# Attention and a gated feed-forward layer on one core: sums of squares in place of maxima, and another planned order

## The chip, the cores and the metric

The kernel runs on one core of one Trainium2 chip. The metric is the device time of one execution in microseconds (us). The engines are TensorE (PE in the rows, its weight loads PEld), VectorE (DVE), ScalarE (ACT), GpSimd (POOL) and SyncE (SP), which issues all transfers of this kernel. Engines run side by side, each takes its own instructions strictly in order, and they wait for one another by semaphores.

## The reference

```python
# q, k, v: (8, 8, 576, 64); f: (8, 8, 576); w_in: (512, 2048); w_out: (2048, 512)
scores = scale * np.matmul(q, k.transpose(0, 1, 3, 2))
cum = np.cumsum(np.log(np.clip(f, 0.0001, 1.0)), axis=-1)
decay = cum[:, :, :, None] - cum[:, :, None, :]
scores = np.where(causal, -1000000000.0, scores + decay)
attn = softmax(scores)                    # row maximum subtracted
out = np.matmul(attn, v)                  # (8, 8, 576, 64)
x = out.transpose(0, 2, 1, 3).reshape(4608, 512)
h = x @ w_in
y = (h * np.cos(h)) @ w_out               # (4608, 512)
```

The weights come as 64-bit floats, the rest as 32-bit floats.

## The kernel before

Work is cut into 32 attention steps, one for each batch and pair of heads (numbers n = 0 to 31), and 16 feed-forward units, two for each batch (320 and 256 tokens). For a pair the kernel computes scores in blocks (L668, L823, L825, L826), adds the mask and takes row minima of the negative (VectorE, L676 or L837), takes exponentials with row sums (ScalarE, L686 or L842), transposes the result (TensorE, L639, for n below 4, by a DMA later), multiplies by v (L713 or L892) and writes x as a high and a low half-precision word (`xh`, `xl`). A unit multiplies x by the first weights in four chunks of four groups (L922, evacuated by ScalarE, L928), applies h cos h (`L937` is the gate's first VectorE operation, a sine on ScalarE follows at L941), and multiplies by the second weights (L968).

Before any of it the weights are prepared. `stage` loads a tile of 128 x 512 64-bit words into a raw buffer (rings `h`, three buffers, for the first weights, and `g`, five buffers, for the second) and makes 32-bit floats of it with three VectorE operations (L472, L476, L480). `bound` sums the absolute values of a tile (ScalarE, L491) and writes the element-wise result, which nobody reads, into a buffer of the ring `ot`. That ring has one buffer, which the outputs and one reduction use too. From the sums `allmax` makes a bound over all partitions (a matmul with ones, L427) and `emit_scale` a power of two by which the tile is scaled and split into two half-precision words (ScalarE L501, VectorE L508). `prep_vscale` does the same for v of each batch: it loads v again in four tiles (ring `stage`, two buffers) and takes the largest absolute value of each with VectorE (L565).

The scores of the first pairs read a buffer of `q32`, loaded from q and k (L609) and from the rows of the decay (L610). For n below 4 this buffer comes out of the ring `g`, so it takes turns with the second weights' tiles. The decay's rows go through DRAM (`cum_d`).

No order is written by hand. Every step is recorded as an operation with an engine, a cost, a priority and the buffers that it reads and writes; a planner (`Plan.order`) simulates the engines and sets one order for each. Its knobs are at the top of the file: `PW1`, `PW2` and `VS0` are priorities of the preparation of the first and second weights and of v of the first batch, `HOLDV`, `HOLDW`, `HOLDX` and `HOLDR` keep loads back until a planned time, and `LEAD` puts the units after their attention. While TensorE is planned to wait, in the first 200 us of the plan, the planner puts in filler matmuls (448 columns, into a bank that is about to be overwritten, L1034), so that it stays busy:

```python
if o.fill and t < FILL:
    a = max([free[e]] + [x.end + 0.25 for x in o.bank])
    if t - a > 0.5:
        o.pads = pe.pad(a, t - 0.2 + PADX)
```

The number of fillers is fixed in the program; how long the wait is on the chip is not.

Of the kernel before, what the change touches and what calls it, by code (L numbers as in the profile page):

```python
# [24 lines left out]
P = 128  # L25
# [11 lines left out]
PW1, PW2 = (-0.95, 1.5, 3.05, 4.0), (2.6, 2.3)  # L37
VS0 = -1.0
# [4 lines left out]
LEAD = 1.0  # L43
HOLDV, HOLDW, HOLDR, HOLDX = 12.0, 20.0, 25.0, 12.0
# [46 lines left out]
PADX = 0.0  # L91
# [42 lines left out]
class Plan:  # L134
# [108 lines left out]
    def forward(self):  # L243
# [8 lines left out]
        t, dma_free, table, span = 0.0, 0.0, None, 0.0  # L252
        pe, port = Clock(), dict.fromkeys(SHARED, 0.0)
        while len(out) < len(self.ops):
# [10 lines left out]
            for e, q in avail.items():  # L265
                if q and free[e] <= t + 1e-9:
# [5 lines left out]
                    if e == "PE":  # L272
                        o.pads = 0
                        if o.fill and t < FILL:
                            a = max([free[e]] + [x.end + 0.25 for x in o.bank])
                            if t - a > 0.5:
                                o.pads = pe.pad(a, t - 0.2 + PADX)
                        end = pe.run(t, o.cost, o.moving)
# [38 lines left out]
def c_act(n, psum=False, aps=0):  # L317
    return (0.052 if psum else 0.093) + n / 1200.0 + 0.093 * aps
# [19 lines left out]
def fox_moe_kernel(ctx: ExitStack, tc: tile.TileContext, qkT, vp, fT, w1, w2, out):  # L338
# [72 lines left out]
    def emit_scale(m2, s, r, u):  # L411
        V.tensor_scalar(m2, m2, float(2.0 ** -40), None, op0=ALU.max)
        V.tensor_scalar(u, m2.bitcast(I32), 0x7F800000, None, op0=ALU.bitwise_and)
        V.tensor_scalar(s.bitcast(I32), u, -1, 268 << 23, op0=ALU.mult, op1=ALU.add)
        V.tensor_scalar(r.bitcast(I32), u, -(14 << 23), None, op0=ALU.add)
# [41 lines left out]

    def stage(w, k, src, pr):

        n = 1024 if wide else 512  # L460
        rb = ring("raw", [P, n], I32, tag=RAWS[w])
        raw = rb.get
        wb = [WB[w, at(w, k) + 1].part(j) for j in range(2)]
# [25 lines left out]
    def bound(w, k, am, ab, pr):  # L489
        junk = ring("junk", [P, 512], BF16, tag="ot")  # L490
        op("ACT", c_act(512, aps=1), lambda: A.activation(junk.get(), wide_of(w, k), AF.Abs, accum_out=am),  # L491
           reads=[WB[w, at(w, k) + 1].part(j) for j in range(2)], writes=[ab, junk], prio=pr)

    def wide_of(w, k):
        return WS_[w][:, at(w, k) + 1].rearrange("p a c -> p (a c)").bitcast(F32)
# [64 lines left out]
    def prep_vscale(b, pr):  # L560
        mx = sm([P, NP], F32, "vmx")
        for p in range(NP):
            st = ring("vst", [P, 640], F32, tag="stage")
            op("SP", T_DGE, lambda st=st, p=p: dma(st.get(), vp[b, p]), writes=[st], prio=pr, size=4 * P * 640, hold=HOLDV * (1 + 2 * b))
            op("DVE", c_dve(640), lambda st=st, p=p: V.tensor_reduce(mx.get()[:, p:p + 1], st.get(), axis=AX.X, op=ALU.max,  # L565
               apply_absolute_value=True), reads=[st], writes=[mx], prio=pr, port=False)
        m1, m2, u = sm([P, 1], F32, "vm1"), sm([P, 1], F32, "vm2"), sm([P, 1], I32, "vu")
        s, r = sm([P, 1], F32, "vs"), sm([P, 1], F32, "vr")
        op("DVE", c_dve(4), lambda: V.tensor_reduce(m1.get(), mx.get(), axis=AX.X, op=ALU.max), reads=[mx], writes=[m1], prio=pr)
        allmax(m1.get, 1, [m1], m2.get, [m2], pr)  # L570
        op("DVE", 0.53, lambda: emit_scale(m2.get(), s.get(), r.get(), u.get()), writes=[m2, s, r], prio=pr)
        vs[b] = (s, r)
# [492 lines left out]
```

## Time and profile before

| | |
|---|---|
| three runs, us | 1089.32, 1091.78, 1100.14 |
| median, us | 1091.78 |
| profiled execution, us | 1095.38 |
| its span, first to last instruction, us | 1093.5 |
[...]
| TensorE, VectorE, ScalarE, GpSimd busy, us | 1057.3, 812.3, 832.3, 180.0 |

The profiled execution is 3.6 us above the median. Busy time counts an instruction of TensorE up to its modelled end, and filler matmuls as work.

### The profile page before, as it was taken

How to read it: one execution, taken by the hardware profiler on the slowest of the kernel's cores; microseconds unless marked ns; L12 is line 12 of the kernel's file. 1: busy time of each engine (PE TensorE's matmuls, PEld its weight loads, DVE VectorE, ACT ScalarE, POOL GpSimd, SP SyncE). 2: the span in 40 equal slices, each digit the busy share in tenths (PEclk: the TensorE clock that was granted, in tenths of full speed). 3: DMA queues.
4: the chain of work that ended last, by engine and by line, in shares of the span. 5: the costliest groups of instructions: out<-in, count | busy, mean ns of one | idle time of the engine just before them, and what ended most of it. 6: DMA issues, size and time to landing. Idle time of an engine off the chain costs nothing. (4 is left out here: it accounts for less than half of the span.)

```text
span 1093.5 us, 23483 instructions
## 1 busy us (share of the span) xinstructions
PE 1057.3 (97%) x8978; PEld 848.6 (78%) x8978; DVE 812.3 (74%) x1790; ACT 832.3 (76%) x1731; POOL 180.0 (16%) x284
## 2 busy tenths in 40 slices
PE   8799997989999999999999999999999999999998
PEld 4587875778777887788778887778778887788787
DVE  5889999778695869778786869677786868762613
ACT  2457899698887979788897979788897979762522
POOL 1000001032213221312212221311222221100000
PEclk9779998999999999999999999999999999999999
DMA  8856334776658465877666565867667564430000
GB/s 289 269 148 220 85 79 102 161 177 124 151 146 197 97 143 116 201 135 147 146 162 167 109 139 120 192 128 164 141 167 163 101 152 96 95 60 20 7 19 20
DMA packets 256279, 146.37 MB, mean 134 GB/s; under 512 B 223336, under 2 KB 231528, under 8 KB 256168
## 3 DMA queue, kind: packets, MB, share of 16 engines
q1 hardware_dynamic: 256168, 144.88, 56.5%
q8 instruction: 70, 1.15, 0.4%
q14 instruction: 41, 0.34, 0.1%
HBM read 72.11 MB, written 10.62 MB: 76 GB/s over the span
## 5 line engine op out<-in xcount | busy, mean ns | idle before, releaser
L968 PE MATMUL hp<-g,W2s 128*128 128x256 f16 (+1 forms) x3072 | 389.4, 287 | 0.0
L922 PE MATMUL hp<-xh,W1s 128*128 128x256 f16 (+1 forms) x2048 | 381.1, 286 | 5.3 <-ACT h L928 5.1
L922 PEld LDWEIGHTS <-W1s 128*128 128x128 f16 x3072 | 294.7, 98 | 83.5 <-issue 7.2
L968 PEld LDWEIGHTS <-W2s 128*128 128x128 f16 x3072 | 297.2, 98 | 75.8 <-issue 0.3
L922 PE MATMUL hp<-xl,W1s 128*128 128x256 f16 (+1 forms) x1024 | 292.6, 286 | 0.0
L863 DVE SCALAR_TENSOR_TENSOR PS<-pa,ri,PS 128x576 f16<-128x576 f32 (+2 forms) x280 | 142.2, 544 | 32.9 <-ACT PS L859 32.3
L842 ACT ACTIVATE pa<-pa,nb 128x448 f32<-128x448 f32 (+2 forms) x280 | 141.5, 506 | 28.1 <-DVE nb L837 22.7
L837 DVE CUSTOM_DVE_ANT_0 pa<-pa,mask 128x448 f32<-128x448 f32 (+1 forms) x280 | 133.4, 505 | 19.7 <-PE pa L826 15.8
L859 ACT ACTIVATE PS<-pa,ri 128x576 f16<-128x576 f32 (+2 forms) x280 | 137.7, 542 | 11.6 <-DVE ri L850 6.0
L847 POOL TENSOR_SCALAR ri<-L 128x1 f32<-128x1 f32 (+1 forms) x168 | 55.7, 331 | 481.8 <-ACT pa L842 460.1
L928 ACT ACTIVATE h<-hp 128x320 f32<-128x320 f32 (+1 forms) x256 | 101.9, 419 | 43.3 <-PE hp L922 42.8
L943 DVE TENSOR_TENSOR h<-h,r 128x1280 f32<-128x1280 f32 (+1 forms) x64 | 87.8, 1371 | 41.9 <-ACT r L941 41.6
L951 DVE TENSOR_TENSOR g<-h,g 128x1280 f16<-128x1280 f32 (+1 forms) x64 | 90.8, 1419 | 22.0 <-ACT g L950 22.0
L939 DVE SCALAR_TENSOR_TENSOR r<-r,m_b,h 128x1280 f32<-128x1280 int32 (+1 forms) x64 | 99.0, 1546 | 1.2
L941 ACT ACTIVATE r<-r,halfpi,m_inv 128x1280 f32<-128x1280 f32 (+1 forms) x64 | 86.2, 1347 | 16.0 <-DVE r L939 15.4
L825 PE MATMUL pa<-QK 128*128 128x288 f32 (+4 forms) x288 | 92.1, 332 | 1.5 <-DVE ri L850 1.3
L771 POOL TENSOR_TENSOR QK<-stage,QK 64x576 fp32r<-64x576 f32 x48 | 76.3, 1590 | 83.1 <-ACT QK L766 47.8
L892 PE MATMUL pa<-pt,vv 128*64 128x256 f16 (+2 forms) x1512 | 78.5, 254 | 9.2 <-DMA pt<-PS 3.9
L950 ACT CAST g<-h 128x1280 f16<-128x1280 f32 (+1 forms) x64 | 74.0, 1157 | 17.1 <-DVE h L943 16.6
L892 PEld LDWEIGHTS <-vv 128*64 128x64 f16 x1512 | 69.4, 110 | 22.0 <-issue 16.5
L937 DVE TENSOR_SCALAR r<-h,m_a 128x1280 int32<-128x1280 f32 (+1 forms) x64 | 54.3, 848 | 43.2 <-ACT h L928 42.3
L826 PE MATMUL pa<-QC 68*128 68x288 f32 (+4 forms) x288 | 76.4, 304 | 0.0
(112 smaller groups left out, 1133.6 us busy)
## 6 DMA issues: line engine op xcount, KB each, us to landing
stage<-in_dram SPq DMA_DIRECT2D x48, 576.0 KB
stage<-in_dram SPq DMA_DIRECT2D x32, 320.0 KB
v<-in_dram SPq DMA_DIRECT2D x32, 320.0 KB
h<-in_dram SPq DMA_DIRECT2D x16, 512.0 KB
g<-in_dram SPq DMA_DIRECT2D x16, 512.0 KB
QC<-QK SPq DMA_DIRECT2D x48, 144.0 KB
out_dram<-ot SPq DMA_DIRECT2D x32, 160.0 KB
out_dram<-ot SPq DMA_DIRECT2D x32, 128.0 KB
```

The source lines that it names most:

```text
L825: T.matmul(c, hi[:, 0, isl], hi[:, 1, d], start=True, stop=False)
L837: op("DVE", c_dve(w) + 0.008, lambda view=view, ib=ib, o=o, w=w, mk=mk, c=c: V.tensor_tensor_reduce(out=view(ib, o, w), in0=view(ib, o, w) ...
L842: op("ACT", c_act(w, True, 2), lambda view=view, ib=ib, o=o, w=w, c=c: A.activation(view(ib, o, w), view(ib, o, w), AF.Exp, bias=nb.get()[ ...
L859: op("ACT", c_act(w, True, 1), lambda view=view, ib=ib, o=o, w=w, c=c, out_=out_: A.activation(out_(0), view(ib, o, w), AF.Copy, scale=ri. ...
L863: op("DVE", c_dve(w) + 0.06, lambda view=view, ib=ib, o=o, w=w, c=c, out_=out_: V.scalar_tensor_tensor(out_(1), view(ib, o, w), ri.get()[: ...
L892: T.matmul(d, vv.get()[:, jb, hd, kv], m, start=first and x == 0, stop=last and x == 2)
L922: T.matmul(hp.get()[:, 0:w_], WS_[1][:, at(1, 4 * c + cb), w, fs], x.get(), start=(n == 0), stop=(n == 11))
L928: op("ACT", c_act(w_, True), lambda hp=hp, k=k: A.activation(h.get()[:, k, 0:w_], hp.get()[:, 0:w_], AF.Copy, scale=float(2.0 ** -24)), re ...
L939: op("DVE", c_dve(N) + 0.045, lambda: V.scalar_tensor_tensor(fl(r), fl(r).bitcast(I32), b1.get()[:, c:c + 1], fl(h), op0=ALU.mult, op1=ALU ...
L943: op("DVE", c_dve(N), lambda: V.tensor_tensor(fl(h), fl(h), fl(r), op=ALU.mult), reads=[r], writes=hk, prio=pr)
L951: op("DVE", c_dve(N), lambda: V.tensor_tensor(gx(1), fl(h), gx(0), op=ALU.subtract), reads=[*hk, gh], writes=[gl], prio=pr, alt=("POOL", 0 ...
L968: T.matmul(po.get()[:, 0:w_], WS_[2][:, at(2, 4 * c + k), w, msl], gh.get()[:, i, k, 0:w_], start=(n == 0), stop=(n == 47))
```

## The change

The element-wise result of a weight tile's sum goes into 256 more words at the end of the tile's own raw buffer, in place of the shared buffer of `ot`. The sum is now one of squares. For the first two batches (`VACT = 2`) the maxima of v on VectorE become sums of squares on ScalarE, with the tile overwritten by its squares, and each tile's result is a part of its own. `emit_scale` halves the exponent where it is given a sum of squares. The planner starts TensorE at 2.5, puts in fillers from a planned wait of 0.3 on and up to its end, and has other priorities and holds. Its order is another from the first instructions on.

```diff
-PW1, PW2 = (-0.95, 1.5, 3.05, 4.0), (2.6, 2.3)
-VS0 = -1.0
+PW1, PW2 = (-0.95, 1.5, 4.05, 3.0), (3.6, 3.3)
+VS0 = 1.5
...
-LEAD = 1.0
-HOLDV, HOLDW, HOLDR, HOLDX = 12.0, 20.0, 25.0, 12.0
+LEAD = 2.5
+HOLDV, HOLDW, HOLDR, HOLDX = 0.0, 0.0, 25.0, 18.0
...
-PADX = 0.0
+PADG, PADE, PE0 = 0.3, 0.0, 2.5
+VACT = 2
...
+        free["PE"] = PE0
...
-                            if t - a > 0.5:
-                                o.pads = pe.pad(a, t - 0.2 + PADX)
+                            if t - a > PADG:
+                                o.pads = pe.pad(a, t - PADE)
...
+        if sq:
+            V.tensor_scalar(m2, m2, float(2.0 ** -80), float(2.0 ** 126), op0=ALU.max, op1=ALU.min)
+            V.tensor_scalar(u, m2.bitcast(I32), 1, 0x7F800000, op0=ALU.logical_shift_right, op1=ALU.bitwise_and)
+        else:
+            V.tensor_scalar(m2, m2, float(2.0 ** -40), None, op0=ALU.max)
+            V.tensor_scalar(u, m2.bitcast(I32), 0x7F800000, None, op0=ALU.bitwise_and)
...
-        rb = ring("raw", [P, n], I32, tag=RAWS[w])
+        rb = ring("raw", [P, n + 256], I32, tag=RAWS[w])
         raw = rb.get
+        raws[w, k] = rb
...
-        junk = ring("junk", [P, 512], BF16, tag="ot")
-        op("ACT", c_act(512, aps=1), lambda: A.activation(junk.get(), wide_of(w, k), AF.Abs, accum_out=am),
-           reads=[WB[w, at(w, k) + 1].part(j) for j in range(2)], writes=[ab, junk], prio=pr)
+        rb = raws[w, k]
+        op("ACT", c_act(512, aps=1), lambda: A.activation(rb.get()[:, -256:].bitcast(BF16), wide_of(w, k), AF.Square, accum_out=am),
+           reads=[WB[w, at(w, k) + 1].part(j) for j in range(2)], writes=[ab, rb], prio=pr)
...
-            op("DVE", c_dve(640), lambda st=st, p=p: V.tensor_reduce(mx.get()[:, p:p + 1], st.get(), axis=AX.X, op=ALU.max,
-               apply_absolute_value=True), reads=[st], writes=[mx], prio=pr, port=False)
+            if b < VACT:
+                op("ACT", c_act(640, aps=1), lambda st=st, p=p: A.activation(st.get(), st.get(), AF.Square, accum_out=mx.get()[:, p:p + 1]),
+                   reads=[st], writes=[mx.part(p), st], prio=pr)
+            else:
+                op("DVE", c_dve(640), lambda st=st, p=p: V.tensor_reduce(mx.get()[:, p:p + 1], st.get(), axis=AX.X, op=ALU.max,
+                   apply_absolute_value=True), reads=[st], writes=[mx.part(p)], prio=pr, port=False)
```

Three places of the order. The changed file's line numbers are higher by 8 to 16 than those before for the same statement.

On SP, ahead of the load of the second head of the first pair, before (`g_395` with L609 and L610 is that load, `h_` and `g_` from `in_3` and `in_4` are weight tiles, `stage_` a tile for v's bound, `cum_d` the decay):

```order
L482 DMA h_311<-in_3_dram 128x1024
L455 DMA cum_d_105<-pt3_136 56x2x576 x2
L482 DMA g_321<-in_4_dram 128x1024
L482 DMA h_361<-in_3_dram 128x1024
L769 DMA QC0_82<-cum_d_105 4x2x576
L769 DMA QC1_83<-cum_d_105 4x2x576
L482 DMA g_381<-in_4_dram 128x1024
L482 DMA h_386<-in_3_dram 128x1024
L564 DMA stage_388<-in_1_dram 128x640
L609 DMA g_395<-in_0_dram 64x2x576
L610 DMA g_395<-cum_d_105 4x2x576
```

The same stretch of SP now (`g_294` is the second head's buffer, `v2_` is v itself):

```order
L493 DMA h_163<-in_3_dram 128x1024
L626 DMA g_112<-cum_d_105 4x2x576
L635 DMA v2_168<-in_1_dram 128x640
L493 DMA g_171<-in_4_dram 128x1024
L575 DMA stage_176<-in_1_dram 128x640
L493 DMA h_181<-in_3_dram 128x1024
L635 DMA v2_281<-in_1_dram 128x640
L625 DMA g_294<-in_0_dram 64x2x576
L626 DMA g_294<-cum_d_105 4x2x576
L625 DMA g_298<-in_0_dram 64x2x576
L626 DMA g_298<-cum_d_105 4x2x576
L448 DMA cum_d_105<-pt3_115 56x2x576
```

The load has moved ahead of the large decay writes and of five weight tiles.

On TensorE, after the first head's scores, before (L668 scores, L427 the reduction of v's bound, L639 transposes):

```order
L668 MATMUL pa1_289<-g_112 128x320
L668 MATMUL pa1_289<-g_112 128x192
L427 LDWEIGHTS ones_78
L427 MATMUL hp_329<-dg_326,ones_78 128x128
L639 MATMUL hp_331<-eyef_76,PS3_84 128x128 x4
L639 MATMUL hp_340<-eyef_76,PS3_84 128x128 x4
```

And now, from the last of 24 fillers (L1050) that follow the first head's scores (L684 scores, L435 the reduction, L655 transposes):

```order
L1050 MATMUL pa1_328<-mask_66,ones_78 128x448
L684 MATMUL pa1_328<-g_294 128x448
L684 MATMUL pa1_328<-g_294 128x64
L684 MATMUL pa2_359<-g_294 128x288 x2
L684 MATMUL pa1_364<-g_294 128x320
L684 MATMUL pa1_364<-g_294 128x192
L684 MATMUL pa1_368<-g_298 128x448
L684 MATMUL pa1_368<-g_298 128x64
L435 LDWEIGHTS ones_78
L435 MATMUL hp_373<-dg_324,ones_78 128x128
L655 MATMUL hp_375<-eyef_76,PS3_84 128x128 x4
```

The second head's scores, which came after the first head's transposes and 33 fillers, now come before the reduction.

On ScalarE, from the start, before (L446 the decay's logarithm, L491 sums of weight tiles, L686 the first exponentials):

```order
L446 ACTIVATE vv_119<-vv_119 64x576
L491 ACTIVATE ot_132,ma_106<-W1s_98 128x512
L491 ACTIVATE ot_150,ma_106<-W1s_98 128x512
L491 ACTIVATE ot_164,ma_106<-W1s_98 128x512
L491 ACTIVATE ot_277,ma_106<-W1s_98 128x512
L686 ACT_TABLE_LOAD
L686 ACTIVATE PS3_84,L_294<-pa1_176,nb_284 128x448
```

And now (L577 the squares of v's tiles, L502 those of weight tiles, L702 the exponentials):

```order
L454 ACTIVATE vv_119<-vv_119 64x576
L577 ACTIVATE stage_121,vmx_138<-stage_121 128x640
L502 ACTIVATE g_117,am2_107<-W2s_99 128x512
L502 ACTIVATE h_125,ma_106<-W1s_98 128x512
L577 ACTIVATE stage_136,vmx_138<-stage_136 128x640
L502 ACTIVATE g_129,am2_107<-W2s_99 128x512
L502 ACTIVATE h_145,ma_106<-W1s_98 128x512
L577 ACTIVATE stage_159,vmx_138<-stage_159 128x640
L502 ACTIVATE g_154,am2_107<-W2s_99 128x512
L502 ACTIVATE h_163,ma_106<-W1s_98 128x512
L702 ACT_TABLE_LOAD
L702 ACTIVATE PS3_84,L_291<-pa1_185,nb_283 128x448
```

Three squares of v and two sums more stand ahead of the first exponential, and tiles of both weights alternate.

## Rows read from the trace of the kernel before

**Rows 1.** The page, busy us, share of the span and instructions of each engine.
```profile
PE 1057.3 (97%) x8978; PEld 848.6 (78%) x8978; DVE 812.3 (74%) x1790; ACT 832.3 (76%) x1731; POOL 180.0 (16%) x284
```

**Rows 2.** Stretches: length, busy us by engine, granted clock, DMA share, GB/s.
```profile
core 0: us, PE busy (x) PEld busy (x) DVE busy (x) ACT busy (x) POOL busy (x), PEclk, DMA share, GB/s
0.00:24.00 24.00, 21.70 (x100) 10.70 (x101) 11.20 (x20) 6.05 (x11) 4.70 (x22) 1.00 0.84 272
44.00:66.00 22.00, 21.66 (x75) 17.08 (x76) 13.10 (x39) 11.41 (x37) 0.51 (x3) 0.53 0.57 207
66.00:131.00 65.00, 62.27 (x438) 52.20 (x436) 63.46 (x190) 50.65 (x145) 3.21 (x15) 1.00 0.55 161
250.00:950.00 700.00, 689.52 (x6209) 562.61 (x6208) 542.07 (x1187) 595.46 (x1203) 152.58 (x205) 1.00 0.64 143
```

**Rows 3.** Order of time, VectorE and ScalarE: start, length, instruction, [idle before].
```profile
203.27 0.74 DVE L937 TENSOR_SCALAR r<-h,m_a 128x1024 int32<-128x1024 f32 x1
...
215.05 0.38 ACT L928 ACTIVATE h<-hp 128x256 f32<-128x256 f32 x1 [3.30 <-PE hp L922]
```

**Rows 4.** Stretches again, each from the span's start.
```profile
0.00:66.00 66.00, 55.50 (x234) 35.86 (x235) 43.26 (x105) 25.54 (x71) 5.51 (x27) 0.79 0.74 245
0.00:131.00 131.00, 117.77 (x669) 88.06 (x670) 106.72 (x295) 76.19 (x215) 8.72 (x42) 0.90 0.65 203
0.00:203.30 203.30, 184.54 (x1178) 136.30 (x1179) 176.95 (x464) 141.80 (x350) 14.98 (x58) 0.92 0.60 170
0.00:215.00 215.00, 196.24 (x1281) 145.05 (x1282) 183.70 (x473) 146.86 (x356) 15.28 (x60) 0.92 0.61 171
```

**Rows 5.** Order of time on TensorE, the first 52 us.
```profile
2.30 21.43 PE L1034 MATMUL pa<-mask,ones 128*128 128x448 bf16 x98 [2.30 <-POOL ones L361]
23.57 2.97 PE L668 MATMUL pa<-g 68*128 68x448 f32 x12
32.02 0.27 PE L427 MATMUL hp<-dg,ones 128*128 128x128 bf16 x1 [5.48 <-DVE dg L424]
...
44.34 6.74 PE L668 MATMUL pa<-g 68*128 68x288 f32 x16 [2.71 <-DMA g<-in_dram]
```

**Rows 6.** Order of time in SP's DMA queue: when loads were issued.
```profile
14.06 0.74 SPq L610 DMA_DIRECT2D g<-cum_d  x1
...
24.36 0.42 SPq L482 DMA_DIRECT2D g<-in_dram  x1
31.43 0.36 SPq L482 DMA_DIRECT2D h<-in_dram  x1
...
36.62 0.59 SPq L609 DMA_DIRECT2D g<-in_dram  x1
```

**Rows 7.** VectorE's groups up to 131 us: count, busy us, mean ns, idle before.
```profile
L476 DVE SCALAR_TENSOR_TENSOR W1s<-h,W1s 128x512 int32<-128x512 int32 x16 | 11.0, 685 | 0.1
...
L472 DVE TENSOR_SCALAR W1s<-h 128x512 int32<-128x512 int32 x16 | 6.9, 432 | 7.0 <-DMA h<-in_dram 7.0
...
L565 DVE TENSOR_REDUCE vmx<-stage 128x1 f32<-128x640 f32 x8 | 6.5, 813 | 0.1
```

**Rows 8.** ScalarE's groups up to 131 us.
```profile
L491 ACT ACTIVATE ot<-W1s 128x512 bf16<-128x512 f32 x16 | 10.2, 636 | 9.5 <-DVE W1s L480 9.3
...
L491 ACT ACTIVATION_READ_ACCUMULATOR ot<-W1s 128x1 f32 x16 | 3.1, 195 | 0.0
```

**Rows 9.** ScalarE's groups, whole span.
```profile
L842 ACT ACTIVATE pa<-pa,nb 128x448 f32<-128x448 f32 (+2 forms) x280 | 141.5, 506 | 28.1 <-DVE nb L837 22.7 <-DVE ri L850 4.5
L859 ACT ACTIVATE PS<-pa,ri 128x576 f16<-128x576 f32 (+2 forms) x280 | 137.7, 542 | 11.6 <-DVE ri L850 6.0 <-DMA pt<-PS 5.2 <-ACT h L928 0.2
...
L941 ACT ACT_TABLE_LOAD x47 | 60.3, 1283 | 0.8
...
L842 ACT ACTIVATION_READ_ACCUMULATOR pa<-pa,nb 128x1 f32 x280 | 58.1, 207 | 0.0
```

**Rows 10.** TensorE's groups, whole span: records, busy us.
```profile
L892 PE MATMUL pa<-pt,vv 128*64 128x256 f16 (+2 forms) x1512 | 78.5, 254 | 9.2 <-DMA pt<-PS 3.9 <-DVE xl L900 3.8 <-DMA QC<-cum_d 1.5
...
L823 PE MATMUL pa<-stage 68*128 68x288 f32 (+4 forms) x96 | 26.2, 414 | 3.8 <-issue 3.8
```

More of the change, by code (lines that the diff above doesn't have):

```diff
@@ L409, in fox_moe_kernel, with emit_scale @@
     w2v = w2.rearrange("(a p) f -> p a f", p=P)
[L411 to L415, printed above, removed]
+    def emit_scale(m2, s, r, u, sq=True):
+        if sq:
[4 more added lines that the diff above has]
+            V.tensor_scalar(u, m2.bitcast(I32), 0x7F800000, None, op0=ALU.bitwise_and)
+        e = 64 if sq else 0
+        V.tensor_scalar(s.bitcast(I32), u, -1, (268 - e) << 23, op0=ALU.mult, op1=ALU.add)
+        V.tensor_scalar(r.bitcast(I32), u, (e - 14) << 23, None, op0=ALU.add)
     def allmax(src, n, reads, dst, writes, pr):
@@ L456, in decay @@
                    reads=[chl.part(0), chl.part(1)], writes=[CD.part((r + 1, k))], prio=-9 + 9.5 * k, size=8 * (h1 - h0) * S, hold=hold)
+    raws = {}
     def stage(w, k, src, pr):
         n = 1024 if wide else 512
-        rb = ring("raw", [P, n], I32, tag=RAWS[w])
+        rb = ring("raw", [P, n + 256], I32, tag=RAWS[w])
         raw = rb.get
+        raws[w, k] = rb
         wb = [WB[w, at(w, k) + 1].part(j) for j in range(2)]
@@ L564, in prep_vscale @@
             op("SP", T_DGE, lambda st=st, p=p: dma(st.get(), vp[b, p]), writes=[st], prio=pr, size=4 * P * 640, hold=HOLDV * (1 + 2 * b))
-            op("DVE", c_dve(640), lambda st=st, p=p: V.tensor_reduce(mx.get()[:, p:p + 1], st.get(), axis=AX.X, op=ALU.max,
-               apply_absolute_value=True), reads=[st], writes=[mx], prio=pr, port=False)
+            if b < VACT:
[4 more added lines that the diff above has]
+                   apply_absolute_value=True), reads=[st], writes=[mx.part(p)], prio=pr, port=False)
         m1, m2, u = sm([P, 1], F32, "vm1"), sm([P, 1], F32, "vm2"), sm([P, 1], I32, "vu")
         s, r = sm([P, 1], F32, "vs"), sm([P, 1], F32, "vr")
-        op("DVE", c_dve(4), lambda: V.tensor_reduce(m1.get(), mx.get(), axis=AX.X, op=ALU.max), reads=[mx], writes=[m1], prio=pr)
+        op("DVE", c_dve(4), lambda: V.tensor_reduce(m1.get(), mx.get(), axis=AX.X, op=ALU.max), reads=[mx.part(p) for p in range(NP)],
+           writes=[m1], prio=pr)
         allmax(m1.get, 1, [m1], m2.get, [m2], pr)
-        op("DVE", 0.53, lambda: emit_scale(m2.get(), s.get(), r.get(), u.get()), writes=[m2, s, r], prio=pr)
+        op("DVE", 0.53, lambda: emit_scale(m2.get(), s.get(), r.get(), u.get(), b < VACT), writes=[m2, s, r], prio=pr)
         vs[b] = (s, r)
```

## The prediction

> **What bounds the kernel now.** I read the page's busy line first [rows 1]: TensorE is busy 97% of the span, VectorE 74%, ScalarE 76%. So the end is set by TensorE's work plus the time in which it does none. Where that time lies is seen in the table of stretches [rows 2]. From 250 to 950 us TensorE is busy 689.5 of 700 us at full clock, so little is to be won there. Up to 205 us VectorE is the full engine once it has work: 63.5 of 65 us from 66 to 131, then 70.2 of 72.3 up to 203.3 [rows 2, 4]. Before 66 us nobody is: VectorE is busy 43.3 of 66 us, ScalarE 25.5 [rows 4]; TensorE looks busy, but its first 21.43 us are 98 filler matmuls [rows 5]. What ends the start is therefore VectorE's work up to about 205 us plus its idle time before 66. To measure it I take the first VectorE operation of the second gate unit (L937, the fifth of its kind), which begins at 203.27 [rows 3]. Up to there VectorE is busy 176.95 us [rows 4], so idle 26.3.
>
> Why it idles early is seen in TensorE's and the DMA queue's order of time [rows 5, 6]. The first head's scores start at 23.57. The reduction of v's bound over partitions stands next in TensorE's order and waits 5.48 us. The second head's scores start only at 44.34. Their load was issued at 36.62: in SP's order it stood behind a weight load that went out at 31.43, 7 us after the one before it at 24.36. [...]
>
> **The change part by part.** *Maxima leave VectorE.* Eight reductions of v, 813 ns each [rows 7], go to ScalarE. Counted in the two orders, seven fewer stand ahead of the L937 place: 7 x 0.813 = 5.7 us less work in a stretch that VectorE bounds. ScalarE's square of 640 columns is not in the trace. The nearest row is the absolute sum of 512 columns, 636 ns and 195 ns for reading the sum [rows 8]; scaled by columns 0.80 + 0.20 = 1.0 us, eight of them 8 us. Most lie ahead of 66 us, where ScalarE idles 40.5 us [rows 4]; what of them returns later is counted below. The weights' squares replace absolute sums one for one, and the scale code keeps its four instructions: no difference.
>
> *Squares beside the words.* A weight tile's junk result goes into its own raw buffer. That frees the one shared buffer in which all 32 sums, one reduction and the outputs took turns. It adds that a raw buffer is free only after ScalarE's sum, at least 0.83 us later [rows 8]; the next weight load waits for that on SP, and behind it every other load. With 3 and 5 buffers the loads run ahead, so I take 0. The upper end is 13 x 0.83 = 10.8 us, if each load that reuses one of the three buffers came last. The lower end is a gain too small to see: the shared buffer tied only ScalarE's own instructions to each other here.
>
> *Order of loads.* The second head's load stands now behind 13 weight tiles, five tiles of v's bound and the four large decay writes; in the new order behind eight, four and none. It then waits only for the first head's scores, whose buffer it takes. These need 2.97 us [rows 5], so it goes out near 26. From issue to first use it took 7.7 us, with other loads ahead (36.62 to 44.34); the new order puts 24 fillers before these scores, 24 x 0.219 (21.43 / 98) = 5.3 us. I expect them between 30 and 34 instead of 44.34. The reduction over v stands behind them, so its 5.48 us wait is covered.
>
> *Start of scores.* [...] Ahead of the first mask VectorE gets two weight tiles more, 0.43 + 2 x 0.685 = 1.8 us each [rows 7], and two maxima fewer: 3.6 - 1.6 = 2.0 us of work moved into a wait. [...] Against that, the read of the decay rows (issued 14.06 [rows 6]) has 704 KB more ahead of it: two weight tiles (512 KB) and one tile of the bound (320 KB) more, two v tiles (320 KB) fewer. At the 272 GB/s of that stretch [rows 2] this is 2.6 us, if the read waits for all of it. [...]
>
> *Idle from 44 to 66.* VectorE idles 8.9 us there [rows 2]. With scores 10 to 14 us earlier and no idle TensorE before them, most of it should go; a pair's chain of scores, mask, exponential, transposes and products stays. I keep 4.0, slightly under half, and count 4.9 won; the ends are 0 and 8.9.
>
> Sum at the L937 place: 5.7 + 3.7 + 4.9 = 14.3 us earlier.
>
> *ScalarE takes some back.* Up to the 21st group evacuated from the first product (215.05 [rows 3]) ScalarE is busy 146.9 us, 76.2 of them up to 131, where that product starts [rows 4]. Counted in the new order it has ahead of that evacuation 8 squares, 7 exponentials, 5 scaled copies, a table load and about 1 us of others more: 8.0 + 7 x 0.71 + 5 x 0.54 + 1.3 + 1 = 18.0 us [rows 9], some 7 of them ahead of the first product. From there it has 70.7 + 11 = 81.7 us to do. At the rate it held from 131 to 203.3, 65.6 of 72.3 or 0.907 [rows 4], that takes 90.1: 131 - 14.3 + 90.1 = 206.8. TensorE has 12 score records and 30 value products more behind it there, 12 x 0.27 + 30 x 0.052 = 4.8 us [rows 10]. The gain at that place is 215 + 4.8 - 206.8 = 13.0. I take this as the sum.
>
> *The rest.* Table loads go from 95 to 103: 8 x 1.28 = 10.3 us on ScalarE [rows 9], which idles 105 of the 700 us from 250 to 950. Thirteen subtractions move from GpSimd to VectorE, which idles 158 there [rows 2]. Cost 0; if TensorE waited for all table loads, 10.3. TensorE's own work is the same (164 fillers for 161). The profiled execution took 1095.4 us, 3.6 above the median, so I take the sum off the median: 1091.8 - 13.0 = 1079.
>
> The table loads measure 1283 ns, and 47 of them have 0.8 us of idle ahead in all [rows 9]: nothing else is lost at a switch. [...]
>
> **The rivals.** *The wait moves on.* In the new SP order the second pair's second head is loaded behind three tiles of v's bound, each waiting for ScalarE's square of an older one. If it comes late in place of the first pair's, TensorE idles again, its clock falls again, and only the maxima are won: 1091.8 - 5.7 = 1086. For it: SP works in order, and 7 us were lost this way before. Against: ScalarE has idle time then.
>
> *All idle goes.* 5.7 + 3.7 + 8.9 + 1.0 (24 to 44, what is left of 22.7) = 19.3: 1072.5. For it: TensorE at full clock throughout. Against: the first pair's chain has little beside it.
>
> [...]
>
> *ScalarE becomes the bound.* It idles 68.1 us up to the 215 us place. If it idles as long with 18.0 us more to do, that place comes at 233.1, with 4.8 us more of TensorE's work done: 13.3 us slower, 1105. It decides from the point where that idle time stays above 54.8. For it: 91% busy at the end of the start already. Against: 40.5 of the 68.1 lie before 66 us, where it waits for the same late scores.
>
> *Table loads on the path.* As a mechanism of this kernel, eight loads for which TensorE waits: 10.3 by the row, 1089. [...]
>
> **How the numbers follow.** Forecast 0.46; the wait moves on 0.25; all idle goes 0.13; scores late 0.06; ScalarE the bound 0.06; table loads 0.04. The range goes down to 1068 (of the 10.5 us that TensorE idles from 250 to 950, four or so may go with another order) and up to 1090, which takes in the moved wait, the table loads and some of the late raw buffers. One per cent, about what a measurement can tell here with runs from 1089.3 to 1100.1, is 1080.9 or 1102.7. Best case and most of the forecast lie below: faster 0.56; slower 0.06; the rest, 0.38, within.
>
> **What would show it.** In the profile after: the second head's scores near 30 to 34; granted clock about 1.0 from there to 66; VectorE idle up to the L937 place about 18 us against 26, and that operation near 189. Wrong, if the clock is at its lower level for 20 us again or the first product still starts near 131: then the wait has moved, and the DMA queue's order of time would name the load. Wrong in size, if TensorE's idle time from 250 to 950 differs by more than 4 us.

## The result, and the profile after

| | before | changed |
|---|---|---|
| first comparison: median of 20 runs each, us | 1092.91 (1085.27 to 1102.05) | 1083.04 (1079.25 to 1092.39) |
| ratio, 95% interval | | 0.991 (0.9885 to 0.9936) |
| repeated on another chip: median, us | 1091.92 (31 runs) | 1085.64 (12 runs) |
| ratio, 95% interval | | 0.9947 (0.9915 to 0.9979) |
| profiled execution; its span; mean granted clock | 1095.38; 1093.5; 0.984 | 1085.19; 1083.4; 0.991 |

The changed kernel is faster by 9.9 us in the first comparison, where 13.0 was forecast, and by 6.3 in the second. Five of before's 31 runs there are slow ones, which the ratio leaves out; the median of the other 26 is 1089.43, 3.8 above the changed kernel's. Between chips a few us are not told apart (before's median is 1091.92 on this second one, 1096.68 and 1096.65 on those of later runs), so below each kernel stands beside before's runs on its own chip.

The busy line of the page after answers to [rows 1]:

```profile
PE 1053.6 (97%) x8981; PEld 843.5 (78%) x8981; DVE 825.9 (76%) x1796; ACT 847.0 (78%) x1754; POOL 166.5 (15%) x271
```

The stretches after, with the columns of [rows 2]; the last three count from the span's start, like [rows 4]:

```profile
0.00:24.00 24.00, 21.70 (x101) 11.43 (x102) 14.85 (x28) 10.27 (x23) 4.99 (x24) 1.00 0.87 293
24.00:44.00 20.00, 19.83 (x124) 14.27 (x122) 18.62 (x62) 15.15 (x53) 0.30 (x2) 1.00 0.85 294
44.00:66.00 22.00, 20.54 (x107) 16.30 (x105) 16.20 (x53) 13.51 (x39) 0.44 (x3) 0.77 0.97 289
66.00:131.00 65.00, 62.53 (x437) 49.76 (x437) 62.16 (x178) 51.48 (x141) 3.44 (x16) 1.00 0.54 144
131.00:205.00 74.00, 66.06 (x506) 47.41 (x504) 66.36 (x151) 63.08 (x124) 6.55 (x15) 0.93 0.49 109
250.00:950.00 700.00, 690.00 (x6210) 562.10 (x6208) 557.70 (x1190) 602.42 (x1212) 138.74 (x195) 1.00 0.63 142
...
0.00:66.00 66.00, 62.08 (x328) 42.00 (x328) 49.67 (x141) 38.93 (x112) 5.73 (x29) 0.92 0.90 292
0.00:194.10 194.10, 180.05 (x1179) 131.70 (x1180) 172.05 (x458) 149.94 (x369) 15.02 (x58) 0.95 0.63 178
0.00:215.00 215.00, 200.67 (x1349) 146.66 (x1350) 184.93 (x488) 161.93 (x395) 18.21 (x64) 0.95 0.63 177
```

From 250 to 950 us TensorE idles 10.0 us, as before (10.5), so all of the gain lies ahead of it. The clock from 44 to 66 is 0.77 instead of 0.53. Up to 66 us VectorE has done 49.7 us of work instead of 43.3, ScalarE 38.9 instead of 25.5.

TensorE's order of time after answers to [rows 5] (L684 scores, L1050 fillers, L908 P times v in half precision, L839 scores of later pairs):

```profile
21.20 2.97 PE L684 MATMUL pa<-g 68*128 68x448 f32 x12
24.01 4.71 PE L1050 MATMUL pa<-mask,ones 128*128 128x448 bf16 x24
28.55 3.89 PE L684 MATMUL pa<-g 68*128 68x448 f32 x16
...
49.80 0.92 PE L1050 MATMUL pa<-mask,ones 128*128 128x448 bf16 x4
51.95 3.66 PE L684 MATMUL pa<-g 68*128 68x288 f32 x12 [1.22 <-DMA g<-in_dram]
55.83 4.04 PE L684 MATMUL pa<-g 68*128 68x448 f32 x8
...
158.93 1.24 PE L839 MATMUL pa<-stage 68*128 68x288 f32 x4 [0.57 <-DVE PS L879]
160.09 0.22 PE L908 MATMUL pa<-pt,vv 128*64 128x64 f16 x1
166.09 1.93 PE L908 MATMUL pa<-pt,vv 128*64 128x64 f16 x23 [5.78 <-DMA pt<-PS]
167.94 4.00 PE L839 MATMUL pa<-stage 68*128 68x448 f32 x8
```

The second head's scores start at 28.55 instead of 44.34, without a wait. The second pair's second head, at 51.95, waits 1.22 us for its load, and then eight score matmuls of 448 columns and less take 4.04 us (clock 0.50 from 56 to 60 us); at a clock of 1.00 eight of the same form take 2.11 (the first set of fillers, below). At 160 us TensorE waits 5.78 us for the transposes of P, and the clock falls once more, to 0.50 from 164 to 172 us. The first feed-forward product starts at 117.94, 12.9 us earlier than before.

The two places of [rows 3], and SP's issues of the two heads' loads, for [rows 6]:

```profile
194.06 0.75 DVE L953 TENSOR_SCALAR r<-h,m_a 128x1024 int32<-128x1024 f32 x1
...
213.35 0.40 ACT L944 ACTIVATE h<-hp 128x256 f32<-128x256 f32 x1
...
17.52 0.59 SPq L625 DMA_DIRECT2D g<-in_dram  x1
18.79 0.65 SPq L626 DMA_DIRECT2D g<-cum_d  x1
...
44.34 0.59 SPq L625 DMA_DIRECT2D g<-in_dram  x1
44.98 0.61 SPq L626 DMA_DIRECT2D g<-cum_d  x1
```

The fifth gate operation comes 9.2 us earlier (203.27 to 194.06), the 21st evacuation 1.7 earlier with 4.8 us more of TensorE's work behind it, together 6.5. VectorE's busy time up to the gate operation fell by 4.9 us, its idle time by 4.3, from 26.3 to 22.05.

### The profile page after: what moved, and what is told of

Its sections match the earlier page's. It is cut to its first block, busy times and chain, and to the rows that moved or that the text cites. A ratio compares the mean times of both kernels' runs of the same rounds, so it can differ in the third digit from the quotient of the medians.

```text
span 1083.4 us, 23496 instructions
## 1 busy us (share of the span) xinstructions
PE 1053.6 (97%) x8981; PEld 843.5 (78%) x8981; DVE 825.9 (76%) x1796; ACT 847.0 (78%) x1754; POOL 166.5 (15%) x271
## 4 chain that ended last, share of the span: by engine, by line
PE 61%; ACT 9%; DMA 3%; DVE 2%; issue 1%; POOL 0%; SPq 0%; ACTq 0%; DVEq 0%; POOLq 0%
PE hp L984 26%; PE hp L938 23%; PE pa L908 5%; PE pa L841 3%; PE pa L842 3%; DMA pt<-PS 2%; ACT pa L858 2%; ACT PS L875 1%; ACT r L957 1%; ACT L858 1%; DMA out_dram<-ot 1%; DVE PS L879 1%; ACT L957 1%; ACT QK L782 1%; ACT h L944 1%
## 5 line engine op out<-in xcount | busy, mean ns | idle before, releaser
L879 DVE SCALAR_TENSOR_TENSOR PS<-pa,ri,PS 128x576 f16<-128x576 f32 (+2 forms) x280 | 140.5, 543 | 26.8 <-ACT PS L875 26.3
L853 DVE CUSTOM_DVE_ANT_0 pa<-pa,mask 128x576 f32<-128x576 f32 (+2 forms) x280 | 131.6, 511 | 28.8 <-PE pa L842 27.5
L875 ACT ACTIVATE PS<-pa,ri 128x576 f16<-128x576 f32 (+2 forms) x280 | 134.7, 542 | 17.2 <-DVE ri L866 8.7
L858 ACT ACTIVATE pa<-pa,nb 128x576 f32<-128x576 f32 (+2 forms) x280 | 140.6, 503 | 9.1 <-DVE nb L853 7.6
L863 POOL TENSOR_SCALAR ri<-L 128x1 f32<-128x1 f32 (+1 forms) x168 | 59.8, 356 | 426.0 <-ACT pa L858 412.0
L967 DVE TENSOR_TENSOR g<-h,g 128x1280 f16<-128x1280 f32 (+1 forms) x61 | 85.3, 1398 | 18.6 <-ACT g L966 18.5
L787 POOL TENSOR_TENSOR QK<-stage,QK 64x576 fp32r<-64x576 f32 x45 | 71.8, 1597 | 173.0 <-issue 110.2
L955 DVE SCALAR_TENSOR_TENSOR r<-r,m_b,h 128x1280 f32<-128x1280 int32 (+1 forms) x64 | 93.9, 1468 | 0.8
L953 DVE TENSOR_SCALAR r<-h,m_a 128x1280 int32<-128x1280 f32 (+1 forms) x64 | 58.6, 916 | 46.8 <-ACT h L944 45.3
L908 PE MATMUL pa<-pt,vv 128*64 128x256 f16 (+2 forms) x1512 | 79.9, 257 | 6.9 <-DMA pt<-PS 6.5
L908 PEld LDWEIGHTS <-vv 128*64 128x64 f16 x1512 | 70.3, 112 | 20.0 <-issue 17.8
L990 ACT ACTIVATE ot<-hp,m_o 128x320 f32<-128x320 f32 (+1 forms) x64 | 32.2, 503 | 66.7 <-PE hp L984 41.7
```

The costliest lines, as they stand in the source:

```text
L853: op("DVE", c_dve(w) + 0.008, lambda view=view, ib=ib, o=o, w=w, mk=mk, c=c: V.tensor_tensor_reduce(out=view(ib, o, w), in0=view(ib, o, w) ...
L858: op("ACT", c_act(w, True, 2), lambda view=view, ib=ib, o=o, w=w, c=c: A.activation(view(ib, o, w), view(ib, o, w), AF.Exp, bias=nb.get()[ ...
L875: op("ACT", c_act(w, True, 1), lambda view=view, ib=ib, o=o, w=w, c=c, out_=out_: A.activation(out_(0), view(ib, o, w), AF.Copy, scale=ri. ...
L879: op("DVE", c_dve(w) + 0.06, lambda view=view, ib=ib, o=o, w=w, c=c, out_=out_: V.scalar_tensor_tensor(out_(1), view(ib, o, w), ri.get()[: ...
L908: T.matmul(d, vv.get()[:, jb, hd, kv], m, start=first and x == 0, stop=last and x == 2)
L955: op("DVE", c_dve(N) + 0.045, lambda: V.scalar_tensor_tensor(fl(r), fl(r).bitcast(I32), b1.get()[:, c:c + 1], fl(h), op0=ALU.mult, op1=ALU ...
```

## The experiments

**Which part carries the gain.** The change has two halves, the code (squares on ScalarE, their place) and the planner's numbers (with the rules for fillers). Each was run without the other.

```diff
 # numbers only: the kernel before with
+PW1, PW2 = (-0.95, 1.5, 4.05, 3.0), (3.6, 3.3)
+VS0 = 1.5
...
+LEAD = 2.5
+HOLDV, HOLDW, HOLDR, HOLDX = 0.0, 0.0, 25.0, 18.0
...
+PADG, PADE, PE0 = 0.3, 0.0, 2.5
...
 # code only: the changed kernel with the old ones in their place
```

> The kernel before with only the numbers of the change (priorities, holds, lead, first filler stretch): maxima stay on VectorE, sums stay absolute sums into the one shared buffer; the planner then puts the second head's load as early as the changed kernel does. Theory one (order and moved maxima each carry a part): the second head's scores near 30 instead of 44, but VectorE keeps 5.7 us of maxima, so 5 to 7 us faster than before, near 1087. Rival A (the order is everything): as fast as the changed kernel, ratio 0.991, near 1083. Rival B (the order is worth little as long as VectorE has the maxima): within 2 us of before, near 1092.

> The changed code with the old numbers: v's squares on ScalarE and the weights' squares beside their words, but the second head's load again behind the weight tiles and the large decay writes. Theory one: its scores start late again (40 to 46 us), so only the moved maxima are won: 3 to 6 us faster than before, near 1088. Rival A (the order is everything): within 2 us of before, near 1093. Rival B (the maxima are everything): as fast as the changed kernel, near 1083.

| | median, us | before, same chip | ratio, 95% interval |
|---|---|---|---|
| numbers only | 1085.94 | 1096.68 | 0.9909 (0.9885 to 0.9932) |
| code only | 1118.02 | 1096.68 | 1.0203 (1.0164 to 1.0242) |

The numbers alone bring all of the gain, as far as it can be told between chips (0.991 and 0.9947 for the changed kernel), with the maxima still on VectorE: rival A of that run. The code alone is 2% slower, which neither the theory nor a rival had. In TensorE's order of numbers only, the second head's scores come at 28.71 and run at a lower clock (0.59 from 24 to 44 us), after the reduction has waited 2.20 us:

```profile
21.42 2.97 PE L669 MATMUL pa<-g 68*128 68x448 f32 x12
26.60 0.22 PE L428 MATMUL hp<-dg,ones 128*128 128x128 bf16 x1 [2.20 <-DVE dg L425]
...
28.71 5.82 PE L669 MATMUL pa<-g 68*128 68x288 f32 x12
```

Its fifth gate operation starts at 191.85. The stretch up to there:

```profile
0.00:191.85 191.85, 173.43 (x1093) 128.86 (x1094) 171.33 (x457) 140.88 (x349) 18.51 (x58) 0.89 0.63 177
```

**Why the code alone is slower.** One of its edits was undone, with the old numbers and the order that the planner then makes: the weights' squares go into the one shared buffer again.

```diff
...
-        rb = ring("raw", [P, n + 256], I32, tag=RAWS[w])
+        rb = ring("raw", [P, n], I32, tag=RAWS[w])
...
-        rb = raws[w, k]
-        op("ACT", c_act(512, aps=1), lambda: A.activation(rb.get()[:, -256:].bitcast(BF16), wide_of(w, k), AF.Square, accum_out=am),
+        rb = ring("junk", [P, 512], BF16, tag="ot")
+        op("ACT", c_act(512, aps=1), lambda: A.activation(rb.get(), wide_of(w, k), AF.Square, accum_out=am),
...
```

> The changed code with the old numbers, but the weights' squares into the one shared buffer: squares of v on ScalarE are then the only change to before besides the order that follows from it. Theory one (with the old numbers, the raw buffers held until ScalarE's square are what made the code alone 2% slower): 1088 to 1096, as before. Rival (ScalarE's squares of v, or the old order around them, cost it): still over 1105.

It took 1088.81 us (before on that chip 1096.65; ratio 0.9932, 0.9909 to 0.9955): the edit, with the order that follows from it, costs some 29 us with the old numbers (20 between the two profiled executions, 1109.26 and 1088.88). Without it the kernel is 7.8 us faster than before, though it has the old numbers and issues the second head's load late, at 33.42 (36.62 before). What it has is the clock: 31 fillers reach up to the second head's scores, where before waited 2.71 us, and the clock from 44 to 66 us is 1.00 instead of 0.53:

```profile
41.79 3.89 PE L683 MATMUL pa<-g 68*128 68x288 f32 x16
...
44.00:66.00 22.00, 20.78 (x139) 16.26 (x138) 21.20 (x63) 18.32 (x58) 0.54 (x4) 1.00 0.83 264
```

So the gain can be had another way than by an early load. Nor does it show a price of the maxima: the kernel before, with fillers alone and the maxima in place, is as fast where its clock holds (the last experiment).

The stretch where the two part, first code only, then the same with the shared buffer:

```profile
86.00:116.00 30.00, 27.27 (x130) 22.51 (x128) 23.55 (x83) 18.79 (x55) 0.15 (x1) 0.66 0.16 51
```

```profile
86.00:116.00 30.00, 28.34 (x200) 23.69 (x198) 29.25 (x102) 25.11 (x75) 2.36 (x11) 1.00 0.21 65
```

ScalarE's order of time and two of the waits (60 to 125 us) of code only:

```profile
79.44 0.63 ACT L501 ACTIVATE g<-W2s 128x512 bf16<-128x512 f32 x1 [0.77 <-DVE W2s L490]
82.09 0.63 ACT L501 ACTIVATE g<-W2s 128x512 bf16<-128x512 f32 x1 [1.92 <-issue]
83.84 0.63 ACT L501 ACTIVATE h<-W1s 128x512 bf16<-128x512 f32 x1 [1.03 <-DVE W1s L490]
```

```profile
POOL g L623 <- ACT g L501: 20.0, 2, 17.8
SPq L492 <- ACT h L501: 6.0, 1, 6.0
```

SP waits 6.0 us with a weight load until ScalarE has squared the tile whose buffer it takes, and GpSimd waits 17.8 us in one piece to clear a score buffer in the ring `g` for the same reason. On ScalarE the squares stand ahead of exponentials and wait for VectorE. With the shared buffer the clearing waits for the scores that used the buffer before, and no wait for a weight tile's squares stands among the longest of that stretch. But GpSimd waits for these buffers as long in sum there (31.5 us, with code only 33.5), so its waiting alone doesn't show the price. The order differs too, since the planner knows of the holding; how much is wait and how much is order was not separated.

**The place of two heads' loads.** In the changed kernel's own order, four loads (two for each head) were moved in SP's queue; `move` takes them out and puts them in ahead of operation 103.

```diff
...
+    move([96, 97, 128, 129], 103)
```

> The changed kernel in its own order, but the loads of the second head and of the next pair's first head moved behind the four large decay writes and two weight tiles in SP's order. Theory one: they go out near 28 instead of 17.5 us, the second head's scores start 5 to 8 us later (34 to 37), TensorE waits for the load and its clock falls: 4 to 8 us slower than the changed kernel, near 1088. Rival (the place of this load does not matter, since VectorE has weights to convert meanwhile): within 2 us of the changed kernel, near 1083.

1091.68 us, ratio 0.9959 (0.9933 to 0.9985), where before took 1096.68. The load went out at 23.32, not at 28, since the tiles ahead of it moved up. Still TensorE waits 3.51 us for it, and the 16 score matmuls take 6.06 us for 3.89:

```profile
23.32 0.59 SPq L625 DMA_DIRECT2D g<-in_dram  x1
...
24.16 4.71 PE L1060 MATMUL pa<-mask,ones 128*128 128x448 bf16 x24
32.37 6.06 PE L684 MATMUL pa<-g 68*128 68x448 f32 x16 [3.51 <-DMA g<-in_dram]
```

The first feed-forward product starts at 125.19, 7.25 us later than in the changed kernel; the profiled span is 8.1 longer (1091.5). The changed kernel itself did not run on this chip; its variant of the next experiment did, at 1084.34, and against that the price is 7.3 us. About half of it is the wait; that the rest is the clock behind it (0.83 from 24 to 44 us, where the changed kernel has 1.00) is the author's estimate: the one run whose mean clock was 0.994 took 1083.80, where the changed kernel at that clock takes 1079.25 to 1081.82.

**The maxima.** In the changed kernel's order v's bounds went back to VectorE, at the places of the squares.

```diff
...
-                op("ACT", c_act(640, aps=1), lambda st=st, p=p: A.activation(st.get(), st.get(), AF.Square, accum_out=mx.get()[:, p:p + 1]),
+                op("ACT", c_act(640, aps=1), lambda st=st, p=p: V.tensor_reduce(
+                   mx.get()[:, p:p + 1], st.get(), axis=AX.X, op=ALU.max, apply_absolute_value=True),
...
-        op("DVE", 0.53, lambda: emit_scale(m2.get(), s.get(), r.get(), u.get(), b < VACT), writes=[m2, s, r], prio=pr)
+        op("DVE", 0.53, lambda: emit_scale(m2.get(), s.get(), r.get(), u.get(), False), writes=[m2, s, r], prio=pr)
...
```

> The changed kernel with the bounds of v taken again as maxima by VectorE (eight reductions), at the places in the order where ScalarE's squares stood; all else the same. Theory one (VectorE bounds the start, each microsecond moved off it counts): the place of the fifth gate operation and the end come 4 to 6 us later, near 1088. Rival (VectorE waits at the start for scores anyway, the maxima fit in): within 1.5 us of the changed kernel, near 1083.

1084.34 us, ratio 0.9895 (0.9866 to 0.9923): no difference from the changed kernel that can be seen, with runs from 1081 to 1089. Of this kernel, the stretch from 44 to 66 us:

```profile
44.00:66.00 22.00, 20.46 (x139) 16.68 (x140) 21.83 (x65) 15.10 (x46) 0.92 (x4) 1.00 1.02 292
```

VectorE is busy 21.83 us here, three maxima (2.4 us) among it. The 16.20 of the changed kernel's profile were measured at a lower clock, 0.77; with the clock held at 1.00 it is 20.05 (the first set of fillers, below), so some 1.8 us more fit into the stretch. In this execution, which took 1089.01, the fifth gate operation stands at 198.68, 4.6 us later than in the changed kernel's profile, as theory one has it. But its clock fell at 75.83 (0.87 from 66 to 131 us), so this profile does not tell the maxima from the clock.

**Fillers at the waits that were left.** Two waits of TensorE stood out in the profile after, at 50 and at 160 us. Fillers were put into each, and into both.

```diff
 # first set: the scores that waited 1.22 and 0.57 us
+    pl_.ops[214].pads, pl_.ops[330].pads = 11, 13
...
 # second set: the product of P and v that waited 5.78 us
+    o = pl_.ops[831]
+    o.pads, o.fill = 28, lambda: pvs[5, 0].get()[:, 0:PAD]
```

> The changed kernel as it is, for comparison on the same chip: 0.989 to 0.994 of before.

> The changed kernel with more fillers on TensorE ahead of the scores of the second pair's second head (11 for 4) and of the third pair's first head (13 for 9), where it waited 1.22 and 0.57 us for a load; nothing else moves. Theory one (the wait after light work drops the clock, and the lower level from 53 to 64 us is on the path): granted clock 1.0 from 44 to 66, 3 to 5 us faster than the changed kernel, and its times less spread. Rival (VectorE and ScalarE set the pace there, fillers only take the place of a wait): within 1 us of the changed kernel.

> The changed kernel with 28 fillers ahead of the product of P and v that waits 5.78 us for the transposes of P at 160 us; nothing else moves. Theory one (the clock that falls in that wait costs the 3.7 us by which the next matmuls are slower): granted clock 1.0 from 166 to 175, 2 to 4 us faster than the changed kernel. Rival (ScalarE, busy throughout from 155 to 185, sets the pace): within 1 us of it.

> Both sets of fillers. Theory one: the two gains add, 5 to 8 us faster than the changed kernel, 0.985 of before. Rival of the first set: only the second's gain; rival of the second: only the first's; both rivals: no difference.

| | median (lowest to highest), us | ratio to before, 95% interval |
|---|---|---|
| changed, again | 1085.64 (1079.68 to 1091.23) | 0.9947 (0.9915 to 0.9979) |
| first set | 1079.77 (1077.38 to 1080.49) | 0.9898 (0.9861 to 0.9935) |
| second set | 1084.03 (1078.90 to 1087.14) | 0.9935 (0.9904 to 0.9967) |
| both | 1080.79 (1079.97 to 1087.92) | 0.9942 (0.9913 to 0.9971) |

The first set wins 5.9 us in the median and takes the spread away: its eight runs all had a mean clock of 0.994 or 0.995, the changed kernel's twelve 0.984 to 0.994. In its profile:

```profile
44.00:66.00 22.00, 21.52 (x148) 17.25 (x149) 20.05 (x61) 16.89 (x51) 0.59 (x4) 1.00 1.02 294
```

```profile
50.42 2.24 PE L1051 MATMUL pa<-mask,ones 128*128 128x448 bf16 x11
52.70 3.08 PE L684 MATMUL pa<-g 68*128 68x288 f32 x12
55.84 2.11 PE L684 MATMUL pa<-g 68*128 68x448 f32 x8
```

The second set keeps the clock for the most part (0.98 from 131 to 205 us, where it was 0.93; it falls once, to 0.50 from 170 to 173.4), and gives little for it, 1.6 us in the median:

```profile
159.59 5.46 PE L1054 MATMUL pa<-mask,ones 128*128 128x448 bf16 x28
165.63 1.08 PE L909 MATMUL pa<-pt,vv 128*64 128x64 f16 x23 [0.43 <-DMA pt<-PS]
170.31 3.09 PE L909 MATMUL pa<-pt,vv 128*64 128x256 f16 x30 [1.56 <-DVE xl L918]
180.90 2.11 PE L840 MATMUL pa<-stage 68*128 68x448 f32 x8 [1.51 <-DVE PS L880]
```

The faster matmuls only wait for VectorE afterwards, 1.56 and 1.51 us: TensorE isn't what the others wait for there. So both sets together are worth no more than the first, which is the fastest version on this chip by its median. The intervals of the four ratios overlap; what tells the first set from the changed kernel is that only two of the latter's twelve runs lie in the range of its eight.

**The small prices, once more.** With the first set the spread is some 3 us, so the maxima and the held raw buffers were priced on top of it, in the same order. In the second run the results of the weights' squares go into one buffer, taken outside of the plan.

```diff
...
-        rb = ring("raw", [P, n + 256], I32, tag=RAWS[w])
+        rb = ring("raw", [P, n], I32, tag=RAWS[w])
...
-        op("ACT", c_act(512, aps=1), lambda: A.activation(rb.get()[:, -256:].bitcast(BF16), wide_of(w, k), AF.Square, accum_out=am),
+        op("ACT", c_act(512, aps=1), lambda: A.activation(junk(), wide_of(w, k), AF.Square, accum_out=am),
...
```

> Maxima of v on VectorE in the changed kernel's order, with the fillers of the run that had 11 and 13 ahead of two loads (1079.8 us, 1077.4 to 1080.5), so that the clock's spread no longer hides a small price. Theory one after the runs so far (VectorE does the maxima in time that it waits anyway): 1079 to 1082. Rival, the prediction's term (each maximum ahead of the fifth gate operation counts): 5.7 us more, 1085.

> The same order and fillers, with the results of the weights' squares going into one shared buffer again, so that a raw buffer is free after VectorE's last conversion. The prediction's term (holding it costs nothing in this order): 1079 to 1081. Rival (loads wait for it): faster, up to 10.8 us, 1069 to 1077.

Maxima on VectorE: 1080.28 us (1079.20 to 1082.42), 0.5 above the first set alone. Shared buffer: 1079.85 (1079.04 to 1080.92), no difference. These two ran on another chip than the first set, so a price of one or two us isn't excluded; on their own chip they differ by 0.4. In the profiles the fifth gate operation stands at 190.55 with the first set, at 192.36 with the maxima back and at 189.85 with the shared buffer. Up to there, with the first set and then with the maxima back:

```profile
0.00:190.55 190.55, 178.22 (x1190) 129.59 (x1191) 171.38 (x458) 149.84 (x369) 14.72 (x58) 0.96 0.64 181
0.00:192.36 192.36, 178.88 (x1190) 129.90 (x1191) 176.87 (x465) 145.08 (x353) 15.35 (x58) 0.96 0.63 180
```

**The kernel before, filled.** Nothing is moved, only fillers added at its two waits of [rows 5].

```diff
...
+    o = pl_.ops[26]
+    o.pads, o.fill = 26, lambda: pms[0].get()[:, 0:PAD]
+    pl_.ops[98].pads = 48
```

> The kernel before, with fillers where TensorE waited at the start: 26 ahead of the reduction of v's bound (5.48 us) and 48 for 33 ahead of the second head's scores (2.71 us); order and loads as they were. Theory one (most of the gain of the change is the granted clock, which falls in these waits): clock 1.0 from 44 to 66, 6 to 9 us faster than before, near 1084, with less spread. Rival (the late load itself sets the pace, whatever the clock): within 3 us of before, near 1091.

1087.86 us (1084.76 to 1100.68) against 1096.65; ratio 0.9958 (0.9924 to 0.9992). Seven of its twelve runs lie from 1084.76 to 1087.94 with a mean clock of 0.995 to 0.998, the others above 1091 with 0.984 to 0.991. The profiled one is of the second kind:

```profile
33.13 9.24 PE L1040 MATMUL pa<-mask,ones 128*128 128x448 bf16 x48
44.33 5.20 PE L671 MATMUL pa<-g 68*128 68x288 f32 x16 [1.96 <-DMA g<-in_dram]
```

Even 48 fillers left 1.96 us to wait, and the clock from 44 to 66 was 0.61. Where it held, the kernel before came to within some 7 us of the changed kernel's best runs without any change of its loads. That the seven held the clock in that stretch is read from their means alone. So part of the gain of the change is clock that it loses less often, and part is the new order itself. The kernels on this chip give an estimate of both: before took 1096.65; the old numbers with the clock held from 44 to 66 us (these seven runs, and the code with the old numbers and the shared buffer) 1084.76 to 1089.60; the new order with the clock held there (the two programs with the first set) 1079.04 to 1082.42. That is some 8 us for each. The new order is more than the early load, so how much of its part is the load's stays open.

## Why the prediction came out right, and where its terms did not

*Where the gain lies* was right: ahead of 205 us, nothing from 250 to 950. *That VectorE bounds the start* was the wrong step. From it followed that each maximum taken from VectorE counts, 7 x 0.813 = 5.7 us. The work did leave (VectorE's busy time up to the gate operation fell by 4.9 us), but the numbers alone reached the changed kernel's ratio with all eight maxima in place, and there VectorE's work up to that place is 171.33 us, 5.6 less than before: the new order puts other work behind the place, so the 4.9 is not the maxima's alone. With the first set of fillers and the maxima back, VectorE is busy 176.87 us up to the gate operation, without them 171.38: of these 5.5 us, 3.7 went into idle time (19.2 us without, 15.5 with them), 1.8 reached the gate operation and 0.5 the end. What the step missed is that this idle time can hold work: VectorE's order has weights to convert beside the pairs' chain, and it was the chain that came late. The sums show that it held 3.7 us; which instructions moved into it was not traced.

*Order of loads* was the right mechanism, at the right place: scores at 28.55 (forecast 30 to 34), the reduction's wait covered. Moving two heads' loads back cost 7.3 us in the median and 8.1 in the span of the profiles. It is not the only way to gain: with the old numbers some 8 us come where the clock holds. One detail was wrong: the load was to wait for the first head's scores and go out near 26. It went out at 17.52, ahead of the start of those scores at 21.20, so it took another buffer than theirs.

*Start of scores* stands in the sum with 3.7 us. VectorE's work makes 2.0 of them; the other 1.7, for the fillers that fall away, are the author's estimate, and no run shows them by themselves. What the runs showed in their place: the first run of fillers took 19.07 us for 89 where 98 took 21.43, the first head's scores began at 21.20, 2.37 earlier, and VectorE's idle time before 24 us fell by 3.65 (12.80 to 9.15). The 704 KB that stood ahead of the decay's rows did not hold the scores back. No row shows the landing: the trace tells only that these rows were there by 21.20.

*Idle from 44 to 66* was mis-sized: 5.8 us are left (22.00 - 16.20) where 4.0 were kept; with the clock held, by the first set of fillers, it is 1.95 (22.00 - 20.05). The granted clock was to be about 1.0 here and was 0.77. Here the rival came in, that the wait moves on: the second pair's second head was issued at 44.34 and waited for 1.22 us. The rival's price stood on all of the order's gain being lost. What was lost is what the first set of fillers gives back, 5.9 us in the median.

*The L937 place*: 9.2 us earlier, forecast 14.3. The start of scores won what was forecast (VectorE's idle time before 24 us is 9.15, where 24 - 11.20 = 12.8 stood), and from 66 to 131 the idle time rose from 1.5 to 2.8. In all it fell by 4.3 us, to 22.05, where the prediction had some 18. The first product still came 12.9 us earlier. Up to the gate operation 3.7 of these were given back: between the two VectorE has 73.04 us of work in the changed kernel and 70.39 before, so some of what it used to do ahead of the first product now lies behind it. *ScalarE takes some back* was too small: 6.5 us at the 21st evacuation, not 13.0, while the end came 10.2 earlier. From the first product to there ScalarE had 82.1 us to do, as forecast (81.7), but took 95.4 for it and not 90.1. The rate taken, 0.907, held up to 203.3 only; up to the evacuation itself ScalarE had been busy 70.8 of 84.2 us before, 0.84, and 0.86 now. From 250 to 950 us the difference of TensorE's idle time is 0.5, and from the gate operation to 250 it idles 1.5 us (2.8 before), so some 2 us of the gain at the end (10.2 - 6.5 - 1.3 - 0.5) are in none of these places; the 4.8 us counted for TensorE's other work may be that much too few, which was not measured.

*The raw buffers, cost 0*: right in the new order (1079.85 and 1079.77). With the old numbers the same edit costs some 29 us, almost three times the bound of 10.8, which counted each hold once and not the score buffers that come out of the same ring. *The table loads, cost 0*: 101 of them in the two large groups at 1283 ns, with 0.9 and 2.0 us of idle ahead in all, and TensorE's steady stretch unchanged.

So that the time fell well inside the range is in part luck. Most of the 5.7 us for the maxima was not there: 0.5 reached the end. Without them the sum is 13.0 - 5.7 = 7.3 us for the order, and measured were 9.9 in the first comparison and 3.8 to 6.3 in the second, so on which side the other terms were off is not told. The outcome with the highest chance, more than one per cent faster (0.56), did not come: 1083.04 lies within one per cent of 1091.78, which had 0.38. The 1079 of the forecast is reached, to 3 us, by the half of the changed kernel's runs with the higher clock, 1079.25 to 1081.53.

## What to carry to other kernels

Before a term is made of work that leaves a busy engine, ask whether its idle time nearby could have held that work: here 3.7 of 5.5 us fitted in, and the end moved by 0.5. Fillers did not always cover the wait that they stood in: here waits of 1.22 to 3.51 us that were left behind them were followed by a lower clock (0.60 in the 12 us behind the first, 0.83 from 24 to 44 us around the last), though not every wait of such a length was (1.51 us in the second set, clock 1.00). So read the wait that is left behind each row of fillers and add to it where others wait for TensorE next. An edit to buffers and a table of priorities that was tuned without it are one change; here the code alone was 2% slower and the numbers alone held all of the gain.

## What the runs showed of the hardware

The spread between runs of one program goes for the most part with the granted clock. Of the changed kernel's first 20 runs, ten had a mean clock of 0.993 or 0.994 and took 1079.25 to 1081.53 us, eight 0.987 to 0.991 and 1084.55 to 1087.38, two 0.984, with 1089.50 and 1092.39; no run took 1083, the median lies between the two groups. On the second chip before goes from 1082.02 at 0.994 to 1097.28 at 0.981 and 1097.50 at 0.984. At the same 0.989 there, before took 1088.62, 1089.29 and 1089.58, the changed kernel 1084.22 to 1086.00, some 4 us less. In the profile of before the clock was 1.00 during the 2.71 us of wait up to 44.34, 0.89 in the 1.36 us behind it and 0.50 from 46 to 64 us. The wait at one place differed from run to run, and the clock with it. The second pair's second head waited 1.22 us in one profile of the changed kernel and 2.08 in another, and the clock fell both times (0.60 and 0.59 in the 12 and 9 us from its start). In the run with the maxima on VectorE, where TensorE's order is the same, it came without a wait, at 52.25, and ran at full clock (1.00 from 44 to 66 us); there the clock fell at 75.83 instead, after 0.77 us. The length of a wait does not settle it in these runs: behind 0.95 us of wait and 4 fillers the same scores saw the clock fall (0.64, second set), behind 0.62 us and 11 fillers it stayed at 1.00 (both sets), and after 1.51 us at 181 us the clock stayed at 1.00 (second set). What the work ahead of a wait has to do with it was not shown: fillers change the wait and that work together.

A lower clock had no fixed price here. Numbers only had 0.982 in the mean (six runs, 0.980 to 0.984) and the changed kernel's time (1085.94 us; the changed kernel again 1085.64); its clock from 24 to 44 us was 0.59. Whether fillers would make that kernel faster than the first set was not tried.
